# Second expert: the mean's small operation folded into scales, and other pairs with 512-column steps in the second product

## The chip, the cores and the metric

The kernel runs on one core of a Trainium2 chip. The metric is the device time of one execution in microseconds (us). The engines are TensorE (PE in the profile: matmul, with its weight loads as PEld), VectorE (DVE), ScalarE (ACT), GpSimd (POOL) and SyncE (SP), which issues the DMAs.

## The reference

A linear attention is followed by two dense experts. The change is in the second, which takes 4,608 tokens of 512 features, in fp32:

```python
h = x @ w_in                                   # 512 -> 1024
h_max = np.max(h, axis=-1, keepdims=True)
e = np.exp(h - h_max)
sm = e / (np.sum(e, axis=-1, keepdims=True) + 1e-09)
solu = h * sm
mu = np.mean(solu, axis=-1, keepdims=True)
var = np.mean((solu - mu) ** 2, axis=-1, keepdims=True)
ln = (solu - mu) / np.sqrt(var + 1e-06) * g_ln
return (ln @ w_out).astype(np.float32)         # 1024 -> 512
```

## The kernel before

The second expert runs from about 850 us to the end. Its 4,608 tokens go through as 18 pairs (`NU = 18`) of two tiles of 128 tokens; `n` is the tile within the pair. Both of its products are Strassen products: seven products of sums of halves in place of eight, each operand split into a high and a low part, so that one product of fp32 precision is three matmuls, high by high (L204), high by low (L205) and low by high (L206). A pair passes through these steps.

- `prep_second` loads the tokens, forms the sums (GpSimd, L779) and splits them into high (ScalarE, L479) and low (GpSimd, L480).
- `second`, the first product: 42 matmuls of 512 columns. Its seven operand products accumulate in a few PSUM banks, and `H_SEED[u]` picks one of three ways to empty these: by additions on VectorE (L1231, and L1236, which takes the row maximum on the way), by copies on ScalarE (L1241, L1281, L1288), or by a mix. With `H_SEED[u]` 0 or 1, one of the banks is the bank called `sums()`, bank 0.
- `soft(u, n)`, in this order: the negated maximum `nmx` (L1309), Exp with the sum `z` (ScalarE, L1314), the product h times e with its sum `sp` (VectorE, L1317), the negated mean `nmp` (VectorE, L1320), the squared small constant `zz` (ScalarE, L1324), the square of the difference from the mean with its sum `v` (ScalarE, L1326), the variance with `zz` (VectorE, L1328), its power of -1/2 `ry` (GpSimd, L1331), `nmp` times `ry` (GpSimd, L1345), and the normalised row (ScalarE, L1347). The division by z is never carried out, since the norm would remove it again; the small constant is scaled with z instead.
- `permute` and `turned` transpose the result: 16 DMAs per pair (L1365), then transposes of 32 x 32 blocks on VectorE (L1392), operand sums (L1403), high part (ScalarE, L1415), low part (VectorE or GpSimd, L1416). The last pair is transposed on TensorE.
- `second_out`, the second product of the pair two before: 7 operand products of 4 blocks. The flat form has three matmuls of 256 columns per block (84 in all), which are drained by additions of 256 columns (L1476) and copies (L1483 on ScalarE, L1481 on VectorE). The wide form, for pairs with `O_WIDE[u]` that are not among the last two (`TAIL`), has one matmul of 512 columns (L1466: high by both weight parts at once) and one of 256 (L1468). Its banks hold two halves that still have to be added: by `wide` (VectorE L1490 over 512 columns, GpSimd L1492 over 256) or by `fold` (VectorE L1496). And its sums are kept by copies on ScalarE, `keep` (L1500); the first of these copies the first bank into bank 0, on which further matmuls accumulate:

```python
prod(bA, A11, B11)
keep(bB, bA)
prod(bC, S3, T3)
prod(bB, S2, T2, more=True)
```

The order of the instructions is decided when the kernel is built. A list scheduler, `Flow`, holds tasks with an engine, a duration out of the code and a due time `at`. At each step it takes the engine that can start first, and there the startable task with the lowest `at`. The instructions are written out in that order, and each engine runs its own in order. The due times come from numbers such as `SOFT_AT`, `E2_LEAD`, `DMA_LAG`, `TURN_LAG` and `OUT_LAG`; on the chip only the order is left of them, and the semaphores.

## Time and profile before

| | |
|---|---|
| Time, median of 3 runs | 1195.18 us (1194.14 to 1196.62) |
| The profiled execution: its time, its span | 1195.32 us, 1193.4 us |
| Granted TensorE clock, mean | 0.998 |
| TensorE busy | 1177.4 us, 99% |
| VectorE, ScalarE, GpSimd busy | 945.2, 861.8, 740.8 us |
| 850 to 1193.4 us: TensorE, VectorE, ScalarE, GpSimd | 338.88, 295.52, 272.64, 211.94 us |

The span runs from the first instruction to the last, and the time has 1.92 us around it. Busy time says how long an engine had an instruction in work, not whether anyone waited for it. Matmuls overlap in the rows (each is shown for some 0.17 us longer than the step to the next), so TensorE's rate is read from start to start. An idle time in a row stands in front of the instruction, with what ended it.

### The profile page before, as it was taken

The page shows a single profiled execution, that of the slowest core. Times are in us where ns is not written, and L with a number is a line of the kernel's source. Part 1 is how long each engine was busy: PE and PEld are TensorE (multiplying, and loading weights), DVE is VectorE, ACT ScalarE, POOL GpSimd, SP SyncE. Part 2 cuts the span into 40 slices and gives each one's busy share as a digit, 9 for nine tenths or more (in the row PEclk, how much of TensorE's full clock was granted, in tenths as well). Part 3 has the DMA queues.
Part 4 walks back from the last instruction along what each step waited for, and adds up shares of the span by engine and source line. Part 5 has one row for each costly group of instructions (what it writes and reads, how often), then busy time and mean ns, then how long its engine had stood idle before and what let it go on. Part 6 is the DMA issues. An engine that isn't in the chain of part 4 may idle for free.

```text
span 1193.4 us, 20361 instructions
## 1 busy us (share of the span) xinstructions
PE 1177.4 (99%) x6678; PEld 1023.4 (86%) x6678; DVE 945.2 (79%) x1631; ACT 861.8 (72%) x1602; POOL 740.8 (62%) x737
## 2 busy tenths in 40 slices
...
GB/s 321 287 364 330 332 319 326 327 271 302 306 200 215 316 275 228 354 302 219 179 353 313 202 206 336 283 247 333 275 108 117 92 134 79 131 100 100 102 94 54
DMA packets 244394, 281.35 MB, mean 236 GB/s; under 512 B 17984, under 2 KB 169536, under 8 KB 244288
## 3 DMA queue, kind: packets, MB, share of 16 engines
...
q8 instruction: 53, 0.87, 0.3%
q14 instruction: 53, 0.43, 0.1%
...
## 4 chain that ended last, share of the span: by engine, by line
PE 90%; DVE 5%; SPq 2%; ACT 1%; DMA 1%; issue 1%; POOL 0%; DVEq 0%; ACTq 0%
PE ps L204 26%; PE ps L206 26%; PE ps L205 26%; PE ps L1466 4%; PE ps L709 3%; PE ps L1468 2%; PE ps L591 2%; SPq L1365 1%; PE ps L741 1%; DMA att<-qkv 1%; DMA xf<-px 1%; DVE mid L1084 0%; DVE rxa L480 0%; DVE ps L1392 0%; DVE fconv L1403 0%
## 5 line engine op out<-in xcount | busy, mean ns | idle before, releaser
L204 PE MATMUL ps<-rg,rwo 128*128 128x512 f32 (+2 forms) x752 | 269.6, 359 | 2.0 <-DVE fh L1084 1.1
L206 PE MATMUL ps<-rg,rwo 128*128 128x512 f32 (+2 forms) x752 | 265.7, 353 | 0.0
L205 PE MATMUL ps<-rg,rwo 128*128 128x512 f32 (+2 forms) x752 | 265.5, 353 | 0.0
L204 PEld LDWEIGHTS ps<-rg,rwo 128*128 128x128 f32 x752 | 141.7, 188 | 20.7 <-DVE mid L1084 2.7
L206 PEld LDWEIGHTS ps<-rg,rwo 128*128 128x128 f32 x752 | 141.7, 188 | 16.3
L480 POOL TENSOR_TENSOR rg<-rawp,rg 128x512 fp32r<-128x512 f32 (+1 forms) x84 | 116.8, 1402 | 62.0 <-ACT rg L479 58.4
L205 PEld LDWEIGHTS ps<-rg,rwo 128*128 128x128 f32 x752 | 141.9, 189 | 15.0
L204 PE MATMUL ps<-rxa,rwi 128*128 128x512 f32 (+1 forms) x384 | 144.8, 377 | 0.0
L206 PE MATMUL ps<-rxa,rwi 128*128 128x512 f32 (+1 forms) x384 | 144.3, 376 | 0.0
L205 PE MATMUL ps<-rxa,rwi 128*128 128x512 f32 (+1 forms) x384 | 144.3, 376 | 0.0
L840 DVE SCALAR_TENSOR_TENSOR fh<-ps,fh 128x512 f32<-128x512 f32 (+1 forms) x126 | 81.0, 648 | 45.7 <-ACT fh L838 44.0
L843 ACT ACTIVATE fh<-fh,const 128x512 f32<-128x512 f32 (+1 forms) x156 | 105.1, 689 | 16.7 <-DVE fh L840 15.6
L204 PE MATMUL ps<-rxb,rwi 128*128 128x512 f32 (+1 forms) x288 | 109.4, 380 | 1.9 <-DVE fh L948 0.9
L205 PE MATMUL ps<-rxb,rwi 128*128 128x512 f32 (+1 forms) x288 | 108.4, 376 | 0.0
L206 PE MATMUL ps<-rxb,rwi 128*128 128x512 f32 (+1 forms) x288 | 108.3, 376 | 0.0
L480 POOL TENSOR_TENSOR ws<-fconv,ws 128x512 fp32r<-128x512 f32 x68 | 83.3, 1228 | 38.6 <-ACT ws L479 32.7
L479 ACT CAST rg<-rawp 128x512 fp32r<-128x512 f32 (+1 forms) x144 | 83.3, 597 | 27.3 <-PE ps L206 18.9
L838 ACT ACTIVATE fh<-ps 128x512 int32<-128x512 f32 (+1 forms) x126 | 70.6, 566 | 44.1 <-PE ps L206 41.8
L779 POOL TENSOR_TENSOR sf<-xf 128x256 f32<-128x256 f32 x72 | 65.5, 909 | 30.5 <-DMA xf<-xd 22.8
L204 PEld LDWEIGHTS ps<-rxa,rwi 128*128 128x128 f32 x384 | 72.1, 188 | 12.1 <-ACT ps L963 0.4
L206 PEld LDWEIGHTS ps<-rxa,rwi 128*128 128x128 f32 x384 | 72.1, 188 | 11.7
L205 PEld LDWEIGHTS ps<-rxa,rwi 128*128 128x128 f32 x384 | 72.1, 188 | 10.8
(197 smaller groups left out, 3122.1 us busy)
## 6 DMA issues: line engine op xcount, KB each, us to landing
...
fh<-e2n SPq DMA_DIRECT2D x256, 64.0 KB, 2.1
...
```

The lines of the kernel that those rows point to most:

```text
L204: PE.matmul(ps, lhsT=lh, rhs=rh, start=start, stop=False, skip_group_check=more)
L205: PE.matmul(ps, lhsT=lh, rhs=rl, start=False, stop=False, skip_group_check=more)
L206: PE.matmul(ps, lhsT=ll, rhs=rh, start=False, stop=stop, skip_group_check=more)
L479: add("ACT", 0.62 if n == 512 else 0.405, lambda: ACT.copy(out=hi(), in_=src()), r=keys, w=hk, at=at)
L480: either(on_dve, n, lambda eng: eng.tensor_tensor(out=lo(), in0=src(), in1=f(hi()), op=ALU.subtract), [*keys, *hk], lk, at)
L591: PE.matmul(buf[bk][e * D:(e + 1) * D, p % 2 * D:(p % 2 + 1) * D], lhsT=k_[:, at_:at_ + D], rhs=k_[:, v_ + at_:v_ + at_ + D], start=(c == ...
L709: PE.matmul(buf[bk][row:row + n, c], lhsT=buf[qs[p]][:, a:a + n], rhs=buf[kvf][:, c], start=True, stop=True)
L779: add("POOL", 0.74, lambda: POOL.tensor_tensor(out=out_(), in0=in0(), in1=in1(), op=fn), r=[*keys, *r], w=w, at=at)
L838: add("ACT", e_(0.6, 0.385, n), lambda: ACT.activation(out=tt().bitcast(I32), in_=h(), func=AF.Copy, scale=INV_2PI, bias=0.25), r=r, w=[tk ...
L840: add("DVE", e_(0.69, 0.418, n), lambda: DVE.scalar_tensor_tensor(out=tt(), in0=h(), scalar=INV_2PI, in1=tt().bitcast(I32), op0=ALU.mult, ...
L843: add("ACT", e_(0.725, 0.509, n), lambda: ACT.activation(out=tt(), in_=tt(), func=AF.Sin, bias=buf["halfpi"][:, 0:1], scale=TWO_PI), r=[tk ...
L1466: PE.matmul(buf[bk], lhsT=hi, rhs=lw_room(b, c // 2)[:, c % 2, :], start=first, stop=False, skip_group_check=True)
```

## The change

It has three parts.

First, other pairs take the wide form of the second product. Before, these were pairs 2, 5, 6, 7, 8, 10, 11 and 13 (pair 17 has the flag but is among the last two); now they are 3 to 15.

Second, the negated mean is no longer formed. The product h times e carries 1 / FP (FP = 1,024) as its scale, so that its sum `sp` is the mean itself and the stored product is smaller by FP. The later scales take that back: Square has the scale -FP and the bias `sp`, the variance the scale 1 / FP^3, the small constant is divided by FP, and GpSimd's last small operation multiplies `sp` by `ry` and -1 / FP. The variance moves from VectorE to GpSimd (`SMALL_POOL[2]`).

Third, numbers of the scheduler: due times of the second expert, `H_SEED` and `O_SEED` (a flat product's choice of banks).

```diff
-E2_LEAD, SOFT_AT, SOFT_D, Q_OFF, CP_D = -33.18, -44.29, -15.08, -0.17, 6.96
+E2_LEAD, SOFT_AT, SOFT_D, Q_OFF, CP_D = 1.52, -76.41, 31.31, -0.17, 6.96
...
-H_SEED = (2, 2, 0, 0, 0, 2, 0, 0, 2, 0, 0, 0, 0, 0, 0, 0, 0, 0)
+H_SEED = (0, 1, 1, 2, 1, 0, 0, 1, 2, 0, 2, 0, 2, 0, 0, 0, 2, 0)
...
-O_WIDE, MM_W = (0, 0, 1, 0, 0, 1, 1, 1, 1, 0, 1, 1, 0, 1, 0, 0, 0, 1), 0.342
+O_WIDE, MM_W = (0, 0, 0, 1, 1, 1, 1, 1, 1, 1, 1, 1, 1, 1, 1, 1, 0, 0), 0.342
...
-PAIR_C, DMA_LAG, TURN_LAG, OUT_LAG = 58.48, 33.18, 71.85, 121.5
+PAIR_C, DMA_LAG, TURN_LAG, OUT_LAG = 46.11, 17.79, 118.53, 95.24
...
+SMALL_POOL = (0, 0, 1)
...
         if n or H_SEED[u] != 1:
-            add("DVE", 0.15, lambda: DVE.tensor_scalar(out=sm("nmx"), in0=sm("mb"), scalar1=-1.0, scalar2=None,
-                                                       op0=ALU.mult), r=[("mb", n)], w=[("nmx", n)], at=at, ps=True)
+            eng, dur = ("POOL", 0.2) if SMALL_POOL[0] else ("DVE", 0.15)
+            add(eng, dur, lambda: (POOL if eng == "POOL" else DVE).tensor_scalar(
+                out=sm("nmx"), in0=sm("mb"), scalar1=-1.0, scalar2=None, op0=ALU.mult),
+                r=[("mb", n)], w=[("nmx", n)], at=at, ps=True)
...
-        add("DVE", 1.3, lambda: DVE.scalar_tensor_tensor(out=buf[hk], in0=buf[hk], scalar=1.0, in1=buf[ek],
+        add("DVE", 1.3, lambda: DVE.scalar_tensor_tensor(out=buf[hk], in0=buf[hk], scalar=1.0 / FP, in1=buf[ek],
...
-        add("DVE", 0.15, lambda: DVE.tensor_scalar(out=sm("nmp"), in0=sm("sp"), scalar1=-1.0 / FP, scalar2=None,
-                                                  op0=ALU.mult), r=[("sp", n)], w=[("nmp", n)], at=at, ps=True)
...
+        add("ACT", 1.24, lambda: ACT.activation(out=buf["junk"], in_=buf[hk], func=AF.Square, scale=-float(FP),
+                                                bias=sm("sp")[:, 0:1], accum_out=sm("v")),
+            r=[hk, ("sp", n)], w=[("v", n), "junk"], at=at)
...
+        def var(eng):
+            return lambda: eng.tensor_scalar(out=sm("v"), in0=sm("v"), scalar1=1.0 / FP ** 3, scalar2=sm("zz")[:, 0:1],
+                                             op0=ALU.mult, op1=ALU.add)
+
+        eng, dur = ("POOL", 0.2) if SMALL_POOL[2] else ("DVE", 0.16)
+        add(eng, dur, var(POOL if SMALL_POOL[2] else DVE), r=[("v", n), ("zz", n)], w=[("v", n)], at=at, ps=True)
...
+        add("POOL", 0.2, lambda: POOL.tensor_scalar(out=sm("nmp"), in0=sm("sp"), scalar1=sm("ry")[:, 0:1], scalar2=-1.0 / FP,
+                                                    op0=ALU.mult, op1=ALU.mult),
+            r=[("ry", n), ("sp", n)], w=[("nmp", n)], at=at, ps=True)
```

Two lines of `soft` use one variable: the function that issues `nmx` reads `eng` when the scheduler runs it, and by then `eng` has been set anew, to "POOL", for the variance. The scheduler has planned `nmx` on VectorE, and the order shows it on GpSimd (L1310) in 32 of the 36 cases; in the other four it is a reduction on VectorE. Lines of the changed kernel stand 1 to 14 lower in the code: Exp is L1316, the product L1319, Square L1331, the variance L1336, the power L1341, `keep` L1510, and from `permute` on every line is 10 further down.

The order at three places shows what moves. The first is the softmax of pair 12. `const_5_73` is the tile with all the small values, `edge_0_133` the one with the maxima, `fconv_0_103` holds h and e, and `ps0_0_169` is bank 0. On GpSimd before:

```order
L779 TENSOR_TENSOR sf_0_107<-xf_0_112 128x256 [waits DMAHW5_49]
L480 TENSOR_TENSOR rwi0_0_731<-sf_1_108,rwi0_0_731 128x512 [waits PE_49,Activation_49]
L779 TENSOR_TENSOR sf_0_107<-sf_0_107,xf_0_112 128x256 [waits DMAHW2_49,Pool_49]
L779 TENSOR_TENSOR sf_0_107<-xf_0_112 128x256
L779 TENSOR_TENSOR sf_0_107<-xf_0_112,sf_0_107 128x256 [waits Pool_49]
L480 TENSOR_TENSOR rwi0_0_731<-xf_1_113,rwi0_0_731 128x256 [waits PE_49,Activation_49]
L1331 TENSOR_TENSOR const_5_73<-const_5_73,const_2_70 128x1 [waits DVE_49]
L1345 TENSOR_TENSOR const_5_73<-const_5_73 128x1 [waits Pool_49]
```

GpSimd in the change, at the same place:

```order
L480 TENSOR_TENSOR rwi0_0_731<-xf_1_113,rwi0_0_731 128x512 [waits PE_49,Activation_49]
L480 TENSOR_TENSOR rwi0_0_731<-sf_1_108,rwi0_0_731 128x512 [waits PE_49,Activation_49]
L1310 TENSOR_SCALAR const_5_73<-edge_0_133 128x1 [waits DVE_49]
L480 TENSOR_TENSOR rwi0_0_731<-sf_1_108,rwi0_0_731 128x512 [waits PE_49,Activation_49]
L1310 TENSOR_SCALAR const_5_73<-edge_0_133 128x1 [waits DVE_49]
L1336 TENSOR_SCALAR const_5_73<-const_5_73 128x1 [waits Activation_49]
L1341 TENSOR_TENSOR const_5_73<-const_5_73,const_2_70 128x1 [waits Pool_49]
L1358 TENSOR_SCALAR const_5_73<-const_5_73 128x1 [waits DVE_49,Pool_49]
```

Two negated maxima (L1310), which wait for VectorE, and the variance (L1336) now stand on GpSimd among the subtractions. ScalarE before, at the two Exps of that pair and the copy into bank 0 (L1500):

```order
L1314 ACTIVATE fconv_0_103,const_5_73<-fconv_0_103,const_5_73 128x1024 [waits DVE_49,Activation_49,Pool_49]
L1324 ACTIVATE const_5_73<-const_5_73,const_1_69 128x1 [waits Activation_49]
L1314 ACTIVATE fconv_0_103,const_5_73<-fconv_0_103,const_5_73 128x1024 [waits DVE_49]
L1500 COPY ps0_0_169<-ps1_0_173 128x512 [waits PE_49]
L1324 ACTIVATE const_5_73<-const_5_73,const_1_69 128x1 [waits Activation_49]
L1326 ACTIVATE fconv_0_103,const_5_73<-fconv_0_103,const_5_73 128x1024 [waits DVE_49]
```

ScalarE in the change:

```order
L1316 ACTIVATE fconv_0_103,const_5_73<-fconv_0_103,const_5_73 128x1024 [waits Activation_49,Pool_49]
L1329 ACTIVATE const_5_73<-const_5_73,const_1_69 128x1 [waits Activation_49]
L1316 ACTIVATE fconv_0_103,const_5_73<-fconv_0_103,const_5_73 128x1024 [waits Pool_49]
L1510 COPY ps0_0_169<-ps7_0_197 128x512 [waits PE_49]
L1331 ACTIVATE fconv_0_103,const_5_73<-fconv_0_103,const_5_73 128x1024 [waits DVE_49]
L1281 COPY fh_0_117<-ps6_0_193 128x512 [waits PE_49]
```

Exp waits for GpSimd in place of VectorE, and the copy into bank 0 (now L1510) still stands behind both Exps here. Over the wide products of the whole kernel, this copy stood ahead of both Exps in 1 case, between them in 4 and behind both in 3; in the change in 1, 7 and 5.

The second place is VectorE at the softmax of pair 12. Before:

```order
L1236 ISA fconv_0_103,edge_0_133<-ps7_0_197,fh_0_117,edge_0_133 128x512 [waits DVE_49,PE_49]
L1236 ISA edge_0_133 128x1
L1309 TENSOR_SCALAR const_5_73<-edge_0_133 128x1 [waits DVE_49]
L1416 TENSOR_TENSOR e2r_1_7847<-ps5_0_189,e2r_1_7847 128x512 [waits Activation_49]
L1236 ISA fconv_0_103,edge_0_133<-ps0_0_169,fh_0_117,edge_0_133 128x512 [waits PE_49]
L1236 ISA edge_0_133 128x1
L1309 TENSOR_SCALAR const_5_73<-edge_0_133 128x1 [waits DVE_49]
L1317 SCALAR_TENSOR_TENSOR fconv_0_103,const_5_73<-fconv_0_103 128x1024 [waits Activation_49]
L1320 TENSOR_SCALAR const_5_73<-const_5_73 128x1 [waits DVE_49,Pool_49]
L1317 SCALAR_TENSOR_TENSOR fconv_0_103,const_5_73<-fconv_0_103 128x1024 [waits Activation_49]
L1320 TENSOR_SCALAR const_5_73<-const_5_73 128x1 [waits DVE_49,Pool_49]
L1328 SCALAR_TENSOR_TENSOR const_5_73<-const_5_73 128x1 [waits Activation_49]
```

VectorE in the change:

```order
L1236 ISA fconv_0_103,edge_0_133<-ps6_0_193,fh_0_117,edge_0_133 128x512 [waits DVE_49,PE_49,Pool_49]
L1236 ISA edge_0_133 128x1
L1426 TENSOR_TENSOR e2r_2_7860<-ps3_0_181,e2r_2_7860 128x512
L1236 ISA fconv_0_103,edge_0_133<-ps0_0_169,fh_0_117,edge_0_133 128x512 [waits DVE_49,PE_49,Pool_49]
L1236 ISA edge_0_133 128x1
L1319 SCALAR_TENSOR_TENSOR fconv_0_103,const_5_73<-fconv_0_103 128x1024 [waits Activation_49]
L1402 STREAM_TRANSPOSE ps2_0_177<-fh_0_117 128x512 [waits DMAHW4_49,DMAHW5_49,DMAHW3_49,DMAHW6_49,DMAHW2_49,DMAHW7_49,DMAHW1_49,DMAHW0_49]
L1319 SCALAR_TENSOR_TENSOR fconv_0_103,const_5_73<-fconv_0_103 128x1024 [waits DVE_49,Activation_49]
L1402 STREAM_TRANSPOSE ps3_0_181<-fh_0_117 128x512
L1506 TENSOR_REDUCE e2n_3_7454<-ps7_0_197 128x256 [waits PE_49]
```

The operations L1309, L1320 and L1328 have left VectorE, and the product of the second tile (L1319) stands behind a transpose that waits for the transfers of `permute`.

The third is TensorE at the second product of pair 3, which was flat. Before, in its first operand product:

```order
L206 MATMUL ps6_0_193<-rxb_0_2622,rwi0_0_731 128x512
L204 MATMUL ps7_0_197<-rg_0_87,rwo_0_77 128x256 [waits DVE_49]
L205 MATMUL ps7_0_197<-rg_0_87,rwo_0_77 128x256
L206 MATMUL ps7_0_197<-rg_0_87,rwo_0_77 128x256
L204 MATMUL ps7_0_197<-rg_0_87,rwo_0_77 128x256
L205 MATMUL ps7_0_197<-rg_0_87,rwo_0_77 128x256
```

TensorE in the change, in the first operand product of the same pair:

```order
L205 MATMUL ps0_0_169<-rxb_0_2622,rwi0_0_731 128x512
L206 MATMUL ps0_0_169<-rxb_0_2622,rwi0_0_731 128x512
L1476 MATMUL ps6_0_193<-rg_0_87,rwo_0_77 128x512
L1478 MATMUL ps6_0_193<-rg_0_87,rwo_0_77 128x256
L1476 MATMUL ps6_0_193<-rg_1_88,rwo_0_77 128x512
L1478 MATMUL ps6_0_193<-rg_1_88,rwo_0_77 128x256
```

Three matmuls of 256 columns per block have become one of 512 and one of 256, and the first product's matmuls (into `ps0`) stand between the blocks. TensorE has 140 fewer instructions in all, 28 for each of five pairs.

## Rows read from the trace of the kernel before

**Rows 1.** The page, busy time: us (share of the span) and instructions.
```profile
PE 1177.4 (99%) x6678; PEld 1023.4 (86%) x6678; DVE 945.2 (79%) x1631; ACT 861.8 (72%) x1602; POOL 740.8 (62%) x737
```

**Rows 2.** Windows: busy us (instructions) of each engine, PEclk, DMA share, GB/s.
```profile
860.00:1180.00 320.00, 318.99 (x1864) 280.81 (x1863) 284.90 (x593) 260.95 (x473) 202.55 (x234) 1.00 0.37 103
```

**Rows 3.** Timeline of TensorE, a flat product's ends: start, duration, instruction, [idle].
```profile
922.48 0.28 PE L204 MATMUL ps<-rg,rwo 128*128 128x256 f32 x1
...
932.55 0.40 PE L204 MATMUL ps<-rxb,rwi 128*128 128x512 f32 x1
```

**Rows 4.** Timeline of TensorE, 24 matmuls of a wide product.
```profile
985.65 0.39 PE L1466 MATMUL ps<-rg,rwo 128*128 128x512 f32 x1
...
989.88 0.40 PE L204 MATMUL ps<-rxb,rwi 128*128 128x512 f32 x1
```

**Rows 5.** Timeline of TensorE around its three longest gaps in the second expert.
```profile
860.46 0.39 PE L206 MATMUL ps<-rxa,rwi 128*128 128x512 f32 x1
861.51 0.50 PE L204 MATMUL ps<-rxb,rwi 128*128 128x512 f32 x1 [0.67 <-DVE edge L1236]
861.85 0.39 PE L205 MATMUL ps<-rxb,rwi 128*128 128x512 f32 x1
...
901.39 0.28 PE L1468 MATMUL ps<-rg,rwo 128*128 128x256 f32 x1
901.86 0.50 PE L204 MATMUL ps<-rxb,rwi 128*128 128x512 f32 x1 [0.19 <-DVE edge L1236]
...
1116.98 0.28 PE L1468 MATMUL ps<-rg,rwo 128*128 128x256 f32 x1
1117.40 0.50 PE L204 MATMUL ps<-rxb,rwi 128*128 128x512 f32 x1
```

**Rows 6.** Groups of VectorE, 800 to 1193.4: busy, mean ns | idle before.
```profile
L1392 DVE STREAM_TRANSPOSE ps<-fh 128x512 f32<-128x512 f32 x64 | 42.6, 706 | 2.2 <-issue 1.4 <-DMA xf<-px 0.5 <-DMA fh<-e2n 0.3
...
L1476 DVE TENSOR_TENSOR fh<-ps,e2n 128x256 f32<-128x256 f32 x25 | 10.4, 418 | 9.4 <-PE ps L206 6.6 <-ACT e2n L1483 2.8
...
L1490 DVE TENSOR_TENSOR e2n<-ps,e2n 128x512 f32<-128x512 f32 x16 | 10.9, 679 | 1.5 <-ACT e2n L1500 1.4
...
L1328 DVE SCALAR_TENSOR_TENSOR const<-const 128x1 f32<-128x1 f32 x36 | 7.0, 202 | 4.1 <-ACT fconv L1326 3.9
...
L1320 DVE TENSOR_SCALAR const<-const 128x1 f32<-128x1 f32 x36 | 5.2, 151 | 2.6
```

**Rows 7.** Groups of ScalarE, the same stretch.
```profile
L1314 ACT ACTIVATE fconv<-fconv,const 128x1024 f32<-128x1024 f32 x36 | 41.4, 1151 | 12.7 <-DVE const L1309 12.4
...
L1500 ACT COPY e2n<-ps 128x512 f32<-128x512 f32 x16 | 9.2, 575 | 1.0 <-PE ps L1468 0.9
```

**Rows 8.** Groups of GpSimd, the same stretch.
```profile
L480 POOL TENSOR_TENSOR rwi<-sf,rwi 128x512 fp32r<-128x512 f32 x35 | 45.4, 1308 | 10.7 <-ACT rwi L479 10.5
...
L1345 POOL TENSOR_TENSOR const<-const 128x1 f32<-128x1 f32 x36 | 6.8, 190 | 2.8
...
L1492 POOL TENSOR_TENSOR fh<-e2n 128x256 f32<-128x256 f32 x8 | 5.9, 741 | 4.8 <-DVE e2n L1490 4.3 <-DVE const L1328 0.4
```

**Rows 9.** Timeline of VectorE ahead of the gap at 860.46.
```profile
857.41 0.47 DVE L1328 SCALAR_TENSOR_TENSOR const<-const 128x1 f32<-128x1 f32 x1
```

**Rows 10.** Timeline of ScalarE, then TensorE, at pair 12: the copy into bank 0.
```profile
1060.93 1.14 ACT L1314 ACTIVATE fconv<-fconv,const 128x1024 f32<-128x1024 f32 x1
...
1062.07 0.58 ACT L1500 COPY ps<-ps 128x512 f32<-128x512 f32 x1
...
1063.07 0.40 PE L1466 MATMUL ps<-rg,rwo 128*128 128x512 f32 x1
```

**Rows 11.** Timeline of GpSimd, then VectorE, at the same place.
```profile
1060.11 0.74 POOL L779 TENSOR_TENSOR sf<-sf,xf 128x256 f32<-128x256 f32 x1
1060.80 1.75 POOL L779 TENSOR_TENSOR sf<-xf 128x256 f32<-128x256 f32 x1
...
1060.73 1.23 DVE L1317 SCALAR_TENSOR_TENSOR fconv<-fconv 128x1024 f32<-128x1024 f32 x1
```

40 lines of the change are left out of this document (18 added, 22 removed).

## The prediction

> **What bounds the kernel now.** I read the page first: TensorE is busy for 99% of the span [rows 1]. Between 860 and 1180 us, which is the second expert almost alone, TensorE is busy for 318.99 of 320 us at the full granted clock (1.00, the 2.4 GHz level); VectorE follows with 284.90, ScalarE with 260.95, GpSimd with 202.55 [rows 2]. The other engines therefore count only by the moments at which TensorE waits for one of them. So I went through TensorE's own timeline for gaps between matmuls. A 256-column matmul takes 0.12 us from start to start (10.07 us for the 84 of one second product [rows 3]) and a 512-column one about 0.23 (a pair of both takes 4.23 / 12 = 0.353 [rows 4]). Against that, three gaps of any size stand in the second expert [rows 5]: 860.46 to 861.51 (1.05 us, so 0.82 too much), 901.39 to 901.86 (0.35 too much) and 1116.98 to 1117.40 (0.30 too much). The matmul behind such a gap is slow as well: 861.51 to 861.85 is 0.34, 0.11 too much, which I take for all three. The first two name a VectorE drain of PSUM (L1236) as releaser. All three together are 1.8 us: this is all that relief of VectorE can be worth at these places.
>
> **The second product in 512-column steps.** A flat product is 7 x 4 x 3 = 84 matmuls of 256 columns, a wide one 28 of 512 and 28 of 256: the same 21,504 columns in 56 instructions. Eight pairs were wide, thirteen are now: five products change. Per twelve flat matmuls the trace has 10.07 / 7 = 1.439 us [rows 3], for the eight that replace them 4.23 / 3 = 1.410 [rows 4]. The difference of 0.029 times 7 operand products times 5 pairs is **-1.0 us**. Only one product of each kind stands behind it, so I keep 0 and -2.0 as bounds.
>
> The Trainium skill ("TensorE: Matmul & The Clock Gate", Back-to-back issue gap) gives an isolated matmul N / 2.4 ns plus some 2.5 ns at the warm clock. By that estimate the 28 instructions saved per product would be worth 28 x 2.5 = 70 ns, 0.35 us for five products in place of 1.0. The trace has 120 ns where this formula has 109, so it is the trace that I follow.
>
> **The same products on the other engines.** On VectorE 29 additions of 256 columns (L1476, 0.418) and a net two more copies turn into 10 additions (L1490) and 10 folds of 512 columns at some 0.68 [rows 6]: -12.1 + 0.8 + 13.6 = +2.3 us. ScalarE gets 15 more copies of 512 columns (L1500, 0.575) and 23 - 10 more in the first product, whose drains were dealt out anew by H_SEED: 28 x 0.575 = 16.1, less 8 short copies [rows 7], so about +13. GpSimd gets 10 additions of 0.741 (L1492) [rows 8]. None of it takes time at these totals, since ScalarE stays near 274 of 320 us and TensorE is at 319.
>
> **The mean.** The operation that made the negative mean (L1320, 36 x 0.151 = 5.4 us) is gone, the variance sum (L1328, 36 x 0.202 = 7.3) goes to GpSimd, and so does, as the order shows, the negated maximum (L1309, of the size of L1320, 32 of 36; the other four become a reduction over 1,024 columns) [rows 6]. VectorE loses 36 x (0.151 + 0.151 + 0.202) = 18.1 us here, +2.3 above, and 18 half-bank operations of the first product (18 x 0.68 = 12.2), less the four reductions at twice 0.68 (5.4): -22.6 us, so 262 of 320. Also gone are its waits ahead of these operations, 4.1 us before L1328 and 2.6 before L1320 [rows 6], which delayed what stood behind. GpSimd gains 68 operations of 0.19 (as L1345 [rows 8]) = 12.9, and 7.4: 223 of 320 us, a share of 0.70.
>
> What is that relief worth? In front of the gap at 860.46 VectorE did a variance sum from 857.41 that took 0.47 instead of 0.20 because it waited, and the drains behind it came late [rows 9]. Without it I take this gap as gone: 0.93 with its slow matmul. The two others (0.35 + 0.30 + 0.22 = 0.87) stand behind runs of half-bank work that the new seeds deal out otherwise; I take half, 0.43. Together **-1.4 us**, bounds 0 and -1.8.
>
> **What the move of the negated maximum adds.** Exp (L1314) waits for that maximum and already stands 12.4 us in all for it [rows 7]. On VectorE it stood directly behind the drain that makes it. On GpSimd, in order, it stands behind whatever GpSimd has begun: at pair 12 a subtraction L480, which takes 1.308 [rows 8]. Behind Exp on ScalarE stands the copy that keeps a product in bank 0 (L1500) and behind that the matmul that writes on there. In pair 12 the second Exp ran from 1060.93, the copy from 1062.07 for 0.58, so to 1062.65, and the first matmul on the kept sum began at 1063.07, only 0.42 us later [rows 10]. If GpSimd is busy with 0.70 and the rest of the operation in front is anything between 0 and 1.3 us, the part beyond 0.42 is on average 0.88 x 0.88 / (2 x 1.3) = 0.30, times 0.70 = 0.21 us per pair. That hits where the copy stands behind both Exps, in 5 of the 13 pairs by the order; where it stands between the two (7), an Exp of 1.14 us is no longer ahead of it, and I take nothing. 5 x 0.21 = **+1.0 us**. And where the maximum stands at the head of GpSimd's queue before the drain is done, the subtractions L480 queued behind it wait too, and after them the first product's matmul with the low part; with 30% of GpSimd's time free I take nothing for it. Bounds: 0, where GpSimd is free in time, and 12 x 0.88 = 10.6, where it always waits out a whole L480.
>
> The order of the permuting transfers and of the VectorE transposes behind them changes as well. VectorE's 64 transposes stood idle for 2.2 us in all, of which 0.8 for transfers [rows 6]. In the change the second half's L1319 stands behind such a transpose at pair 12, and behind it that half's Square, norm and permute. I put it at nothing, since both results are wanted two pairs later only, and keep its loss as a rival.
>
> **Sum.** -1.0 - 1.4 + 1.0 = -1.4 us against the profiled execution's 1195.32 (span 1193.4 and 1.92 around it): 1193.9. The median of the runs is 0.14 below the profiled one, which changes nothing.
>
> **Rivals.**
> *The relief is whole, and GpSimd is free.* All 1.8 us of gaps go, the maximum costs nothing: -1.0 - 1.8 = -2.8, so 1192.5 or somewhat less. For it: VectorE falls from 89% to 82% of the window, and Exp no longer queues behind VectorE's other work. Against it: the gaps are three accidents of order, and a new order may have others.
> *The maximum on GpSimd delays what stands behind it (the other side).* If Exp comes late by enough that the kept bank comes 0.43 us late in each of 12 pairs, TensorE stands 5.2 us more, and with the 1.0 saved and no relief the time is 1199.5. It is slower by over 0.2% (2.4 us, which is about what a measurement of this kernel can tell from no change) from (2.4 + 1.0) / 12 = 0.28 us per pair. For it: GpSimd's additions (L779) take 0.74 at 1060.11, but 1.75 at 1060.80, when VectorE's two-input product L1317 began at 1060.73 [rows 11]. A maximum for the second half that is ready just there, behind such an operation, would wait out the product too. Against it: ScalarE has other work to do meanwhile, and 7 of 13 copies moved ahead of the second Exp.
> The Trainium skill ("SBUF — State Buffer", Who interferes with whom) says of the same: a VectorE operation with two SBUF inputs and a GpSimd operation that reads SBUF exclude each other for a whole instruction. The trace agrees, 0.74 against 1.75; by it the delay would be the rest of the product, up to 1.2 us.
> *The gain is given back at the transposes.* If VectorE stands for late permutes by 0.13 us in each of 18 pairs and TensorE behind it, the 2.4 us saved are gone: 1195.2.
>
> **How the numbers follow.** The forecast has 0.40; its own range is 1192.3 to 1195.5 (0.07 of it below the bound for faster, 0.33 within). The whole relief has 0.33, all faster. The late maximum has 0.15, 0.13 of it slower and 0.02 within. The transposes have 0.12: 0.10 within, 0.02 slower. So faster 0.40, same 0.45, slower 0.15. The range of 1191.2 to 1197.4 takes in the forecast, the transposes, most of the whole relief (with two us saved by the wide products instead of one) and the late maximum where it costs up to 0.25 us per pair.
>
> **What would show it.** Twelve flat matmuls replaced by eight at 1.41; TensorE's gaps of 0.82, 0.35 and 0.30 gone or elsewhere; VectorE near 262 us in the window; negated maxima on GpSimd that begin up to 1.3 us behind the drain; ScalarE's idle time before Exp above 12.4 us; the copy into bank 0 ending closer than 0.42 to its matmul, and gaps on L1476 where it ends behind. The prediction is wrong if such gaps, or new ones behind transposes and casts, sum to more than 3.5 us, or if the wide products save more than 0.06 us for each twelve.

## The result

The changed kernel takes 1202.57 us (median of 4 runs, 1200.74 to 1202.75), the kernel before in the same comparison 1194.66 (1193.57 to 1196.62): ratio 1.0063, interval 1.0050 to 1.0076, so 7.9 us slower. The profiled execution is the quickest of the four (1200.74 us, span 1199.0), 1.8 below the median. In nine of the sixteen profiled executions of this document, that of the kernel before among them but not that of the changed one, TensorE's granted clock is 0.50 (the 1.2 GHz level) for 3.4 us near 26 us, which makes them some 1.6 us longer. The kernel before in its window from 26 to 29 us:

```profile
26.00:29.00 3.00, 3.00 (x26) 2.36 (x25) 2.37 (x6) 1.63 (x5) 0.00 (x0) 0.50 1.05 325
```

The same window of the changed kernel has 1.00; from 20 to 25 us TensorE was busy for 3.23 us in both, so what sets the clock there stays open. So traces are compared from 740 us on: from the 4,201st matmul, the same one in all these orders, to the last, TensorE takes 449.3 us before and 456.9 in the change. That is 7.5 us of the 7.9.

### The profile after

The page's busy times, against [rows 1]:

```profile
PE 1179.3 (98%) x6538; PEld 1014.7 (85%) x6538; DVE 925.8 (77%) x1499; ACT 873.5 (73%) x1622; POOL 759.0 (63%) x815
```

The windows from 860 to 1180 us, against [rows 2]:

```profile
860.00:1180.00 320.00, 316.07 (x1678) 267.67 (x1679) 264.23 (x467) 269.04 (x486) 218.28 (x304) 1.00 0.38 107
```

The other engines came out as forecast: VectorE 264 us (forecast 262, before 285), ScalarE 269 (274), GpSimd 218 (223). TensorE is busy for 316.1 of 320 us in place of 319.0 and gets through less in it (685,056 columns against 695,808), at the same granted clock (1.00, the 2.4 GHz level). So the time went into waits of TensorE, which the next lines look for.

The term for the wide products came out as well. From TensorE's timeline, the first of 24 matmuls of a wide product and the one behind the last:

```profile
924.13 0.39 PE L1476 MATMUL ps<-rg,rwo 128*128 128x512 f32 x1
...
928.36 0.40 PE L1476 MATMUL ps<-rg,rwo 128*128 128x512 f32 x1
```

4.23 us for 24, so 1.41 for eight as in [rows 4]: five products save their 1.0 us. What else happens is in the gaps. I took each step of TensorE from start to start, from 780 us on, and summed what it has over the normal step (0.226 us after 512 columns, 0.120 after 256, 0.109 after 128), where that is above 0.025. The kernel before has 3.0 us of this and the changed one 11.1.

The groups of ScalarE, Exp, against [rows 7], and of GpSimd, the negated maximum and the last small operation:

```profile
L1316 ACT ACTIVATE fconv<-fconv,const 128x1024 f32<-128x1024 f32 x36 | 41.3, 1148 | 15.6 <-POOL const L1310 14.3 <-POOL rwo L1426 0.7 <-DVE const L1314 0.3
```

```profile
L1310 POOL TENSOR_SCALAR const<-edge 128x1 f32<-128x1 f32 x32 | 10.1, 315 | 12.6 <-DVE edge L1236 11.2 <-DVE edge L1257 0.8 <-DMA fh<-e2n 0.3
...
L1358 POOL TENSOR_SCALAR const<-const 128x1 f32<-128x1 f32 x36 | 9.4, 260 | 3.8
```

ScalarE's idle time before Exp has gone from 12.7 to 15.6 us, 14.3 of it for GpSimd. What that does is seen at single places. The timeline of GpSimd, VectorE, ScalarE and TensorE around 853 us:

```profile
850.05 1.30 POOL L480 TENSOR_TENSOR rwi<-sf,rwi 128x512 fp32r<-128x512 f32 x1
851.31 1.21 POOL L1310 TENSOR_SCALAR const<-edge 128x1 f32<-128x1 f32 x1
...
850.01 0.75 DVE L1236 CUSTOM_DVE_ANT_0 fconv<-ps,fh,edge 128x512 f32<-128x512 f32 x1 [0.30 <-issue]
...
850.69 1.74 DVE L1319 SCALAR_TENSOR_TENSOR fconv<-fconv 128x1024 f32<-128x1024 f32 x1
...
852.56 1.15 ACT L1316 ACTIVATE fconv<-fconv,const 128x1024 f32<-128x1024 f32 x1 [1.54 <-POOL const L1310]
...
853.70 0.58 ACT L1241 COPY ps<-ps 128x512 f32<-128x512 f32 x1
...
853.12 0.40 PE L206 MATMUL ps<-rxa,rwi 128*128 128x512 f32 x1
854.33 0.50 PE L204 MATMUL ps<-rxa,rwi 128*128 128x512 f32 x1 [0.82 <-ACT ps L1241]
```

The maximum of the second half, ready when VectorE's drain L1236 ended at 850.76, stood behind a subtraction until 851.31 and then took 1.21 us, where the others take about 0.23: VectorE's product with two SBUF operands (L1319) had run since 850.69, and both ended at 852.4 to 852.5. ScalarE stood idle for 1.54 us before Exp, the copy into bank 0 behind it ended at 854.28, and TensorE had the gap: 0.99 us, and 0.11 in the slow matmul behind. Three of the 32 maxima on GpSimd (at 851.31, 984.94 and 1125.17) took 1.11 to 1.21 us, each while such a product ran, the other 29 took 0.21 to 0.27. The Trainium skill ("SBUF — State Buffer", Who interferes with whom) says that a VectorE instruction with two SBUF inputs contends with a GpSimd instruction that reads SBUF; this trace agrees (1.21 against 0.23).

The same engines around 1085 us, without VectorE:

```profile
1082.36 1.30 POOL L480 TENSOR_TENSOR rwi<-sf,rwi 128x512 fp32r<-128x512 f32 x1 [0.60 <-ACT rwi L479]
1083.63 0.23 POOL L1310 TENSOR_SCALAR const<-edge 128x1 f32<-128x1 f32 x1
...
1083.89 1.15 ACT L1316 ACTIVATE fconv<-fconv,const 128x1024 f32<-128x1024 f32 x1 [1.61 <-POOL const L1310]
...
1085.37 0.58 ACT L1510 COPY ps<-ps 128x512 f32<-128x512 f32 x1
1085.88 1.14 ACT L1316 ACTIVATE fconv<-fconv,const 128x1024 f32<-128x1024 f32 x1
...
1085.42 0.28 PE L1478 MATMUL ps<-e2r,e2r 128*128 128x256 f32 x1
1086.00 0.50 PE L1476 MATMUL ps<-rg,rwo 128*128 128x512 f32 x1 [0.30 <-ACT ps L1510]
```

Here no such product ran. The maximum waited out a subtraction of 1.30 us, Exp began at 1083.89, the copy ended at 1085.95, and TensorE's matmul on the kept sum began 0.46 us late, with a slow step behind it. The trace has six gaps behind a late Exp (853, 946, 987, 1007, 1085, 1164): 2.7 us with their slow matmuls. At the last of them (0.15) GpSimd was idle, and the maximum ran as soon as VectorE's drain had ended. Four of them (946, 1007, 1085, 1164) stand where the copy is between the two Exps of a pair, as it is at 1085.37 above, and one (987) where it is behind both.

### The profile page after: what moved, and what is told of

The parts are those of the page before. It is cut to its first block, busy times and chain, and to the rows that moved or that the text cites. A ratio compares the mean times of both kernels' runs of the same rounds, so it can differ in the third digit from the quotient of the medians.

```text
span 1199.0 us, 20054 instructions
## 1 busy us (share of the span) xinstructions
PE 1179.3 (98%) x6538; PEld 1014.7 (85%) x6538; DVE 925.8 (77%) x1499; ACT 873.5 (73%) x1622; POOL 759.0 (63%) x815
## 4 chain that ended last, share of the span: by engine, by line
PE 89%; DVE 4%; ACT 3%; POOL 1%; issue 1%; DMA 1%; SPq 0%; ACTq 0%; DVEq 0%; POOLq 0%
PE ps L204 25%; PE ps L206 25%; PE ps L205 25%; PE ps L1476 6%; PE ps L1478 3%; PE ps L709 3%; PE ps L591 2%; PE ps L741 1%; ACT fconv L1316 1%; DMA att<-qkv 1%; DVE mid L1084 0%; ACT e2n L1361 0%; DVE rxa L480 0%; DVE rxb L480 0%; SPq L1375 0%
## 5 line engine op out<-in xcount | busy, mean ns | idle before, releaser
L204 PE MATMUL ps<-rg,rwo 128*128 128x512 f32 (+2 forms) x672 | 246.7, 367 | 1.9 <-DVE mid L1084 0.8
L206 PE MATMUL ps<-rg,rwo 128*128 128x512 f32 (+2 forms) x672 | 243.2, 362 | 0.6 <-DVE rwo L1426 0.6
L205 PE MATMUL ps<-rg,rwo 128*128 128x512 f32 (+2 forms) x672 | 242.8, 361 | 0.0
L480 POOL TENSOR_TENSOR rg<-rawp,rg 128x512 fp32r<-128x512 f32 (+1 forms) x84 | 116.0, 1392 | 62.3 <-ACT rg L479 59.7
L204 PEld LDWEIGHTS ps<-rg,rwo 128*128 128x128 f32 x672 | 126.4, 188 | 20.3 <-DVE mid L1084 2.2
L206 PEld LDWEIGHTS ps<-rg,rwo 128*128 128x128 f32 x672 | 126.4, 188 | 16.9 <-DVE rwo L1426 0.8
L205 PEld LDWEIGHTS ps<-rg,rwo 128*128 128x128 f32 x672 | 126.5, 188 | 14.8
L480 POOL TENSOR_TENSOR ws<-fconv,ws 128x512 fp32r<-128x512 f32 x68 | 83.8, 1236 | 38.5 <-ACT ws L479 32.3
L479 ACT CAST rg<-rawp 128x512 fp32r<-128x512 f32 (+1 forms) x144 | 83.5, 597 | 25.0 <-PE ps L206 20.2
L462 POOL TENSOR_TENSOR fconv<-fconv 128x512 int32<-128x512 int32 x40 | 53.5, 1338 | 43.4 <-DVE fconv L455 34.6
```

What stands on the lines that cost most here:

```text
L204: PE.matmul(ps, lhsT=lh, rhs=rh, start=start, stop=False, skip_group_check=more)
L205: PE.matmul(ps, lhsT=lh, rhs=rl, start=False, stop=False, skip_group_check=more)
L206: PE.matmul(ps, lhsT=ll, rhs=rh, start=False, stop=stop, skip_group_check=more)
L462: add("POOL", 1.3, lambda: POOL.tensor_tensor(out=buf[wk].bitcast(I32), in0=buf[yk].bitcast(I32), in1=buf[wk].bitcast(I32), op=ALU.add), r ...
L479: add("ACT", 0.62 if n == 512 else 0.405, lambda: ACT.copy(out=hi(), in_=src()), r=keys, w=hk, at=at)
L480: either(on_dve, n, lambda eng: eng.tensor_tensor(out=lo(), in0=src(), in1=f(hi()), op=ALU.subtract), [*keys, *hk], lk, at)
```

## The experiments

Theory 1 puts the loss down to the negated maximum on GpSimd, theory 2 to the new order itself. Each run is timed in five rounds against the kernel before on the same chip. The intervals of the ratios are 1 to 2 us wide to either side, so a difference of under 2 us between two runs is shown by their traces or not at all.

### The maximum taken back: a_nmx_dve

```diff
-            add(eng, dur, lambda: (POOL if eng == "POOL" else DVE).tensor_scalar(
+            add(eng, dur, lambda eng=eng: (POOL if eng == "POOL" else DVE).tensor_scalar(
```

> The changed kernel with the negated maximum back on VectorE, in the place where its scheduler had planned it; the order of TensorE, ScalarE and the DMAs stays that of the change word for word. Theory 1 (the maximum on GpSimd makes Exp and the copy into bank 0 behind it late): the loss of 7.5 us goes, and with the 1.0 saved by the wide products the time is 1193 to 1195, ratio to the kernel before 0.998 to 1.001. Theory 2 (the new order itself, its first-product copies L1241 and due times, stalls TensorE): it stays at 1200 or more, ratio 1.005.

Measured: 1198.9 us (1197.91 to 1200.54), ratio 1.0034 (1.0022 to 1.0046). It lies between the two. Each against the kernel before of its own comparison, the maximum on GpSimd costs 7.9 - 4.4 = 3.5 us, and 4.4 stay. The intervals leave the 3.5 anything from 1 to 6; by the traces from the 4,201st matmul on it is 2.4 (456.9 - 454.4), and by the gaps 2.7. The group of Exp on ScalarE:

```profile
L1316 ACT ACTIVATE fconv<-fconv,const 128x1024 f32<-128x1024 f32 x36 | 41.3, 1148 | 6.8 <-DVE const L1310 5.2 <-POOL rwo L1426 0.6 <-DVE ps L1413 0.3
```

Exp's idle time falls to 6.8 us, and the six gaps are gone. Others remain. From the timelines of this run, TensorE at pair 8, then ScalarE and TensorE near the end:

```profile
978.73 0.39 PE L206 MATMUL ps<-rxa,rwi 128*128 128x512 f32 x1
979.79 0.50 PE L204 MATMUL ps<-rxa,rwi 128*128 128x512 f32 x1 [0.68 <-ACT fh L1241]
...
1165.19 1.15 ACT L1331 ACTIVATE fconv<-fconv,const 128x1024 bf16<-128x1024 f32 x1
...
1166.34 1.23 ACT L1361 ACTIVATE e2n<-fconv,const 128x1024 f32<-128x1024 f32 x1
1167.47 0.56 ACT L1510 COPY e2n<-ps 128x512 f32<-128x512 f32 x1
...
1166.74 0.28 PE L1478 MATMUL ps<-rg,rwo 128*128 128x256 f32 x1
1168.09 0.50 PE L1476 MATMUL ps<-e2r,e2r 128*128 128x512 f32 x1 [1.07 <-ACT e2n L1510]
```

At 978.73 the first product of pair 8 (H_SEED 2) goes on in the bank that it has just filled, which ScalarE must copy first: 0.84 us over the normal step. At 1166.74 the wide product of pair 15 goes on in bank 0, and the copy that keeps it (L1510) stands behind Square and the normalised row: 1.23 us.

### The maximum moved in the old order: b_nmx_pool

```diff
-            add("DVE", 0.15, lambda: DVE.tensor_scalar(out=sm("nmx"),
+            add("DVE", 0.15, lambda: POOL.tensor_scalar(out=sm("nmx"),
```

> The kernel before with its 36 negated maxima issued on GpSimd where its scheduler planned them on VectorE; nothing else moves. Theory 1: the loss appears here as well, 4 to 8 us, ratio 1.003 to 1.007, with TensorE's gaps behind the copy into bank 0. Theory 2: within 2 us of before, ratio 0.999 to 1.002.

Measured: 1196.6 us (1195.31 to 1197.56), ratio 1.0014 (1.0005 to 1.0022): 2.1 us slower, less than theory 1 asked for, at the edge of what theory 2 allowed. GpSimd, VectorE and ScalarE at 851, then VectorE and TensorE at 860, then ScalarE and TensorE at 965:

```profile
850.55 1.12 POOL L1309 TENSOR_SCALAR const<-edge 128x1 f32<-128x1 f32 x1 [0.33 <-DVE edge L1236]
...
850.38 1.22 DVE L1317 SCALAR_TENSOR_TENSOR fconv<-fconv 128x1024 f32<-128x1024 f32 x1
...
851.70 1.15 ACT L1314 ACTIVATE fconv<-fconv,const 128x1024 f32<-128x1024 f32 x1 [0.84 <-POOL const L1309]
...
857.66 0.69 DVE L1403 TENSOR_TENSOR fconv<-ps,fconv 128x512 f32<-128x512 f32 x1 [0.61 <-ACT fconv L1427]
...
858.92 0.39 PE L206 MATMUL ps<-rxa,rwi 128*128 128x512 f32 x1
860.79 0.50 PE L204 MATMUL ps<-rxb,rwi 128*128 128x512 f32 x1 [1.49 <-DVE edge L1236]
...
962.09 1.15 ACT L1314 ACTIVATE fconv<-fconv,const 128x1024 f32<-128x1024 f32 x1 [1.60 <-POOL const L1309]
...
964.38 0.57 ACT L1500 COPY ps<-ps 128x512 f32<-128x512 f32 x1
...
964.54 0.40 PE L206 MATMUL ps<-rxb,rwi 128*128 128x512 f32 x1
965.00 0.50 PE L1466 MATMUL ps<-rg,rwo 128*128 128x512 f32 x1
```

The gap of [rows 5] grows from 0.82 to 1.65. The way there leads through ScalarE: the maximum at 850.55 took 1.12 us while VectorE's product L1317 ran, Exp began behind it at 851.70, and after Exp come the squares, the normalised row (L1347) and a copy (L1427), for which VectorE's four half-bank operations ahead of the drain still wait 0.61 us at 857.66. At 964.54 Exp, behind an idle time of 1.60, delays the copy into bank 0, and a gap of 0.23 is new. The move costs 2.1 us in this order (1.7 by the traces) and 3.5 in the new one (2.4); that the order around it makes the difference is not shown, since the intervals overlap.

### The folded mean in the old order: b_fold and b_fold_v

Both take the folded mean and keep the order of TensorE, ScalarE and the DMAs (the place of the removed operation stays in the plan, empty). b_fold also has the variance on GpSimd.

```diff
-        add("DVE", 0.15, lambda: DVE.tensor_scalar(out=sm("nmp"), in0=sm("sp"), scalar1=-1.0 / FP, scalar2=None,
-                                                  op0=ALU.mult), r=[("sp", n)], w=[("nmp", n)], at=at, ps=True)
+        add("DVE", 0.15, lambda: None, r=[("sp", n)], w=[("nmp", n)], at=at, ps=True)
...
-        add("DVE", 0.16, lambda: DVE.scalar_tensor_tensor(out=sm("v"), in0=sm("v"), scalar=1.0 / FP, in1=sm("zz"),
+        add("DVE", 0.16, lambda: POOL.tensor_scalar(out=sm("v"), in0=sm("v"), scalar1=1.0 / FP ** 3, scalar2=sm("zz")[:, 0:1],
```

> The kernel before with the folded mean and the variance on GpSimd, but the negated maximum still on VectorE, and the order of TensorE, ScalarE and the DMAs kept as it was. By the relief term of the prediction VectorE's waits ahead of the gap at 860 go: 0 to 1.8 us saved, ratio 0.9985 to 1.000. By theory 2 no loss either. If small operations on GpSimd cost anything by themselves, it is slower.

Measured: 1194.9 us (1193.54 to 1200.29), ratio 1.0008 (0.9998 to 1.0018): no difference is shown, and the gain that the relief term asked for is not there. The gaps at 901 and 1117 are gone, and the one at 860 has grown. ScalarE, VectorE and TensorE there:

```profile
859.85 1.24 ACT L1347 ACTIVATE e2n<-fconv,const 128x1024 f32<-128x1024 f32 x1 [0.75 <-POOL const L1344]
...
861.12 0.69 DVE L1236 CUSTOM_DVE_ANT_0 fconv<-ps,fh 128x512 f32<-128x512 f32 x1 [0.55 <-ACT e2n L1347]
...
860.26 0.39 PE L206 MATMUL ps<-rxa,rwi 128*128 128x512 f32 x1
861.88 0.50 PE L204 MATMUL ps<-rxb,rwi 128*128 128x512 f32 x1 [1.23 <-DVE edge L1236]
```

The drain L1236 now waits 0.55 us for the normalised row (L1347), since it writes where that one still reads. And that one comes 0.5 us later than in the kernel before, whose row is this, as variance, power and product now all stand on GpSimd among its additions:

```profile
859.38 1.24 ACT L1347 ACTIVATE e2n<-fconv,const 128x1024 f32<-128x1024 f32 x1
```

> The kernel before with the folded mean alone: the operation for the negative mean is gone, the variance and the negated maximum stay on VectorE, and the order of TensorE, ScalarE and the DMAs is kept. By the relief term of the prediction, 0 to 1.8 us faster, ratio 0.9985 to 1.000. By the reading of the run with the variance on GpSimd, in which the gap at 860 grew because the norm came 0.5 us later, the gap at 860 is 0.83 or less here and those at 901 and 1117 go: 0.3 to 0.9 us faster.

Measured: 1193.52 us (1192.36 to 1194.52), ratio 0.9993 (0.9984 to 1.0002): 0.9 us faster, as expected, though the interval still holds 1. TensorE at 860:

```profile
860.21 0.39 PE L206 MATMUL ps<-rxa,rwi 128*128 128x512 f32 x1
861.19 0.50 PE L204 MATMUL ps<-rxb,rwi 128*128 128x512 f32 x1 [0.59 <-DVE edge L1236]
```

0.75 us over the normal step; the gaps at 901 and 1117 are gone, as in b_fold. So by the gaps it is the removed operation that helps, 0.7 us in all, and the variance on GpSimd gives that back at 860 (1.39 in place of 0.75). The times agree with it, but their intervals overlap.

Why the gap at 860 stays is seen in the kernel before. Behind the variance sum of [rows 9], which ended at 857.88, VectorE went on with this:

```profile
858.37 0.69 DVE L1403 TENSOR_TENSOR fconv<-ps,fconv 128x512 f32<-128x512 f32 x1 [0.48 <-ACT fconv L1427]
```

It stood idle for 0.48 us more, for a copy on ScalarE (L1427) that comes behind the squares and a normalised row there. From then on it has no pause up to the drain. In b_fold_v it waits 0.68 us for that copy. The variance's wait was covered by a longer one.

### Other lists of wide pairs in the kernel before: b_wide13, b_wide_mid, b_wide_9_14, b_wide_9

```diff
-O_WIDE, MM_W = (0, 0, 1, 0, 0, 1, 1, 1, 1, 0, 1, 1, 0, 1, 0, 0, 0, 1), 0.342
+O_WIDE, MM_W = (0, 0, 0, 1, 1, 1, 1, 1, 1, 1, 1, 1, 1, 1, 1, 1, 0, 0), 0.342
...
+O_WIDE, MM_W = (0, 0, 1, 1, 1, 1, 1, 1, 1, 1, 1, 1, 1, 1, 0, 0, 0, 0), 0.342
...
+O_WIDE, MM_W = (0, 0, 1, 0, 0, 1, 1, 1, 1, 1, 1, 1, 0, 1, 1, 0, 0, 0), 0.342
...
+O_WIDE, MM_W = (0, 0, 1, 0, 0, 1, 1, 1, 1, 1, 1, 1, 0, 1, 0, 0, 0, 1), 0.342
```

> The kernel before with the change's list of wide pairs alone (3 to 15), planned anew by the scheduler with the old due times. By the term of the prediction 1.0 us saved by five more wide products, ratio 0.999, if its new order brings no gaps. By theory 2, in which an order decides by its own accidents, it can be a few us slower, with new gaps behind the copies into bank 0.

Measured: 1198.83 us (1197.72 to 1201.0), ratio 1.0036 (1.0024 to 1.0048): 4.3 us slower, by this list alone. The saving is there, the new order costs more.

> The kernel before with wide products for pairs 2 to 13, so four more in the middle and none at the end. Theory 1: what cost 4.3 us in the run with pairs 3 to 15 were the last two (gaps of 1.0 at 1112.3, 1.2 at 1152.7, and 1.5 at 1160.9 to 1166.9), so it is 0.5 to 1 us faster than before: ratio 0.999 to 1.000. Theory 2 (a wide product costs wherever it is put): about 2 us slower, ratio 1.002.

Measured: 1198.66 us (1197.99 to 1200.1), ratio 1.0036 (1.0023 to 1.0048). Both expectations missed: it is not the end alone, and 4.6 us is more than theory 2 said. VectorE and TensorE at the largest gap:

```profile
1053.28 0.69 DVE L1403 TENSOR_TENSOR ps<-ps,fconv 128x512 f32<-128x512 f32 x1
1053.88 0.68 DVE L1490 TENSOR_TENSOR e2n<-ps,e2n 128x512 f32<-128x512 f32 x1
1054.48 0.68 DVE L1403 TENSOR_TENSOR fconv<-fconv,ps 128x512 f32<-128x512 f32 x1
1055.07 1.41 DVE L1231 TENSOR_TENSOR fh<-ps,fh 128x512 f32<-128x512 f32 x2
...
1054.46 0.40 PE L206 MATMUL ps<-rxa,rwi 128*128 128x512 f32 x1
1055.81 0.50 PE L204 MATMUL ps<-rxa,rwi 128*128 128x512 f32 x1 [0.96 <-DVE fh L1231]
```

TensorE's order at this place says why:

```
4969 L204 MATMUL ps0_0_169<-rxa_0_82,rwi0_0_731 128x512
4970 L205 MATMUL ps0_0_169<-rxa_0_82,rwi0_0_731 128x512
4971 L206 MATMUL ps0_0_169<-rxa_0_82,rwi0_0_731 128x512
4972 L204 MATMUL ps0_0_169<-rxa_1_83,rwi0_0_731 128x512 [waits DVE_49]
```

Two operand products of the first product stand one behind the other in bank 0 (`ps0`), and between them VectorE has to empty the bank (L1231), behind the sums L1403 and an addition. I read it so that a wide product keeps its sums in bank 0 too, and pushes the first product's shares of that bank together. This became theory 3: a bank written twice running, with a drain between, costs TensorE about 1 us. I counted such places in the orders of the second expert: none in the kernel before, 3 in b_wide13, 4 in b_wide_mid, 2 in the changed kernel, 5 in a_seed_b, 4 in a_tail_seed (both below).

> The kernel before with two more wide products, pairs 9 and 14, chosen by the order alone: in it TensorE never writes two blocks in a row into one bank with a drain between them, which it does four times with pairs 2 to 13 wide and three times with 3 to 15. Theory 3 (each such repeat costs TensorE the length of the drain and its queue, 0.84 to 1.23 us, and nothing else is wrong with wide products): no gap near 1 us appears and the time is 0 to 0.5 us below before, ratio 0.999 to 1.001. If wide products cost by themselves, some 0.8 us each as in the two runs before: 1196 and above, ratio 1.0013 or more.

Measured: 1200.04 us (1199.03 to 1202.03), ratio 1.0050 (1.0036 to 1.0063). Theory 3's time is missed by far, and the time alone would fit wide products that cost by themselves. But up to 1166 us no gap is new, as theory 3 has it; the loss stands at the end. ScalarE and TensorE there:

```profile
1166.28 1.24 ACT L1347 ACTIVATE e2n<-fconv,const 128x1024 f32<-128x1024 f32 x1 [0.52 <-POOL const L1345]
...
1166.26 0.28 PE L206 MATMUL ps<-ws,e2r 128*128 128x256 f32 x1
1168.71 0.71 PE L1380 MATMUL ps<-const,e2n 128*128 128x128 f32 x4 [2.17 <-ACT e2n L1347]
```

TensorE's order now puts the transposes of the last pair ahead of the second product of pair 16, and they wait for the normalised row: 2.33 us, and 2.26 for the next four at 1169.09. Behind these two waits the granted clock is 0.50 (the 1.2 GHz level) up to 1176 us, which adds some 2 us to TensorE's steps.

> The kernel before with one more wide product, pair 9, and pair 14 flat; no bank is written twice running with a drain between. If the loss of the run with 9 and 14 (5.6 us) stood at the end alone, as its two gaps of 2.3 us say, the time is that of before or up to 0.5 us below, ratio 0.999 to 1.001. If a wide product in the middle costs by itself, 1195.5 or above.

Measured: 1194.38 us (1192.97 to 1196.77), ratio 1.0000 (0.9991 to 1.0008). One more wide product in the middle costs nothing. Its 0.2 us are too little to be told.

### The end and the seeds of the changed kernel: a_tail_flat, a_seed_b, a_tail_seed

These three and the next two also have the edit of a_nmx_dve.

```diff
-O_WIDE, MM_W = (0, 0, 0, 1, 1, 1, 1, 1, 1, 1, 1, 1, 1, 1, 1, 1, 0, 0), 0.342
+O_WIDE, MM_W = (0, 0, 0, 1, 1, 1, 1, 1, 1, 1, 1, 1, 1, 1, 0, 0, 0, 0), 0.342
...
-H_SEED = (0, 1, 1, 2, 1, 0, 0, 1, 2, 0, 2, 0, 2, 0, 0, 0, 2, 0)
+H_SEED = (2, 2, 0, 0, 0, 2, 0, 0, 2, 0, 0, 0, 0, 0, 0, 0, 0, 0)
```

> The changed kernel with the negated maximum on VectorE (1198.9 us) and pairs 14 and 15 flat again, as before the change; its plan is the same up to the product of pair 14. In the run with the maximum on VectorE the product of pair 15, which has no first product left to stand between its blocks, shows gaps of 0.17, 1.23 and 0.11 behind the kept sums. Theory 1 (wide products at the end are exposed): these go, and 1.5 to 2.5 us with them, less 0.4 for two flat products: 1197 to 1198. Theory 2 (the loss is in the seeds and due times): 1199 or more.

Measured: 1197.56 us (1196.4 to 1199.2), ratio 1.0028 (1.0018 to 1.0038): 0.9 us back (4.4 - 3.5), the gaps of pair 15 are gone. The intervals overlap; by the traces from the 4,201st matmul on it is 1.6. 3.5 us of loss stay, by the medians and by the traces.

> The changed kernel with the negated maximum on VectorE and the H_SEED of the kernel before, planned anew. Theory 1 (end): the time stays within 1 us of 1198.9. Theory 2 (the copies L1241 of the pairs with seeds 1 and 2, behind which TensorE stood 0.84, 0.63 and 0.76 at 978.7, 1017.3 and 863.8): these gaps go, 2 us or more faster, 1197 or below.

Measured: 1205.69 us (1204.97 to 1206.66), ratio 1.0095 (1.0080 to 1.0111). Both missed. The old seeds do take the old gaps away, but in this order they bring one of 4.0 us at 859 and five of 0.94 to 1.23 at the five repeats. The large one is no repeat: TensorE waits for a cast of the first product's operand on ScalarE (L479). Behind it the granted clock is low for a while:

```profile
863.00:866.00 3.00, 2.84 (x7) 2.29 (x8) 1.38 (x6) 2.55 (x6) 2.90 (x3) 0.50 0.31 76
```

At 0.50, the 1.2 GHz level, matmuls of 512 columns step by 0.43 us in place of 0.226, which costs 1.5 us more.

> Both of the last two at once: pairs 14 and 15 flat, H_SEED of before, the maximum on VectorE. If both theories hold side by side, the savings add up and the time is 1195 or less. If it stays above 1197, the due times of the first expert's end and of the second are what is left.

Measured: 1204.3 us (1203.38 to 1205.24), ratio 1.0081 (1.0069 to 1.0094). The savings do not add up. The flat end saves 1.4 against a_seed_b (1.5 by the traces); the gap of 4.0 us stays.

### Two orders picked by their repeats: a_nmx_plan, a_lag

```diff
-SMALL_POOL = (0, 0, 1)
+SMALL_POOL = (1, 0, 1)
...
-PAIR_C, DMA_LAG, TURN_LAG, OUT_LAG = 46.11, 17.79, 118.53, 95.24
+PAIR_C, DMA_LAG, TURN_LAG, OUT_LAG = 46.11, 17.79, 118.53, 91.24
```

> The change with its scheduler told that the negated maximum runs on GpSimd, planned anew. If the loss of that move (3.7 us) came from the plan not knowing of it, the time is 1199 or less. By theory 3 it is not: the new order has five repeats of a bank with a drain between, against two in the change, so three more gaps of about 1 us, 1203 or above if nothing else falls away.

Measured: 1206.54 us (1205.7 to 1207.61), ratio 1.0104 (1.0090 to 1.0118). Slower, as theory 3 said; the five repeats have gaps of 0.84 to 1.34. A sixth, at 865.72, where both operand products read the same tile (`rxb`), has 1.21; and three places that are none have 0.95, 1.73 and 1.33 (863, 1174, 1179). That the scheduler knows where the maximum runs is no help.

> The changed kernel with the negated maximum on VectorE and pairs 14 and 15 flat (1197.6 us), and one due time of the second product (OUT_LAG) 4 us earlier, planned anew. Its order has four repeats of a bank with a drain between, against one. Theory 3: three more gaps of 0.8 to 1.2 us, 1199.5 to 1201. If repeats do not decide, within 1 us of 1197.6.

The lines of a_tail_flat are in this run too. Measured: 1215.21 us (1213.82 to 1217.01), ratio 1.0177 (1.0163 to 1.0191). The time that theory 3 gave is missed by 14 us. The four repeats have their gaps, 0.84 to 0.85 each, but 14 us more come from others: three of 1.55 before bank 0's kept sum, one of 3.2 at the end. So each repeat has its gap, and theory 3 says nothing of other places; 4 us in one due time moved the time by 17 us.

### The two that help, together: b_fold_w9

The edits of b_fold_v and b_wide_9.

> The same with the folded mean, all small operations left on VectorE: the 0.9 us of the run b_fold_v and the 0.2 us of one wide product add up, ratio 0.998 to 0.9995. If one takes the other's cover away, 1.000 or above.

Measured: 1192.95 us (1192.13 to 1195.04), ratio 0.9991 (0.9982 to 0.9999). It is the fastest of all: 1.5 us below the kernel before by the medians, 1.1 by the ratio, which is just clear of no change, and 0.6 by the traces from the 4,201st matmul on, about as much as b_fold_v (0.7). That the two edits add up is not shown.

## Why the prediction was wrong

**The step that failed** is the order. The prediction asked of the new due times and seeds only what they do to the three old gaps ("the new seeds deal out otherwise; I take half"), and let a new order's own gaps stand as a remark against a rival ("a new order may have others"). No term of the sum had them, although the part on the change showed that most of the second expert was planned anew. They are the largest term: with the maximum back on VectorE 4.4 us are still lost (a_nmx_dve), 5.4 with the 1.0 that the wide products save. The prediction's own sign of being wrong, new gaps of more than 3.5 us, came about. All kernels, sorted by time (TensorE's excess from the profiled execution, as above):

| kernel | median against before, us | excess, us | repeats |
|---|---|---|---|
| b_fold_w9 | -1.5 | 2.5 | 0 |
| b_fold_v | -0.9 | 2.3 | 0 |
| b_wide_9 | 0.0 | 3.0 | 0 |
| before | 0 | 3.0 | 0 |
| b_fold | +0.4 | 2.9 | 0 |
| b_nmx_pool | +2.1 | 4.6 | 0 |
| a_tail_flat | +3.5 | 6.4 | 1 |
| b_wide13 | +4.3 | 8.1 | 3 |
| a_nmx_dve | +4.4 | 8.5 | 2 |
| b_wide_mid | +4.6 | 8.7 | 4 |
| b_wide_9_14 | +5.6 | 9.4 | 0 |
| changed kernel | +7.9 | 11.1 | 2 |
| a_tail_seed | +10.2 | 13.4 | 4 |
| a_seed_b | +11.6 | 15.4 | 5 |
| a_nmx_plan | +12.1 | 16.4 | 6 |
| a_lag | +20.8 | 23.7 | 4 |

The excess, less 3.0 and what the wide products save, gives every time to within 0.8 us. All 31 repeats of these orders have a gap, of 0.84 to 1.34 us; that they come from the wide products' sums in bank 0 is a reading of the order, not shown by itself.

Term by term:
- Wide products, -1.0: right as a rate (1.41 for eight).
- Relief of VectorE, -1.4: in the old order the removed operation gives 0.9 (b_fold_v; 0.7 by the gaps, and not clear of noise), as the gaps at 901 and 1117 go. The gap that I took as gone, at 860, stays at 0.75. The wait was misread: behind the variance sum VectorE stood 0.48 us longer for ScalarE's copy L1427. With the variance on GpSimd the normalised row, which reads what the drain overwrites, is later and the gap longer (1.39 in b_fold). That step was wrong, and the whole relief with it (rival 1).
- The maximum on GpSimd, +1.0: the mechanism was right, the size and the places were not. It costs 3.5 us (2.4 by the traces). It was priced by half an L480 in the 5 of 13 pairs with the copy behind both Exps; of these one has a gap (987, 0.33 with its slow matmul). The 7 pairs with the copy between the Exps were put at nothing, since "an Exp of 1.14 us is no longer ahead of it"; but the first Exp still is, and four of them have gaps (1.2 together). I had given the wait behind L1319 to the rival only, and the first product's copies (853, 1.1) to nobody. Rival 2, which named that wait, had 5.2 for all of it.
- Transposes on VectorE (rival 3): VectorE's idle time before them is 1.4 us, before 2.2; nothing was given back there.
- The busy times of the other engines came out as forecast, but that bore on nothing: none of them was the limit.

So of the 7.9 us, 3.5 are the maximum's by the medians (2.4 by the traces), shown by a_nmx_dve, and 0.9 (1.6) those of the wide products at the end, whose gaps are gone in a_tail_flat. The remaining 3.5 (with the 0.6 that three wide products save, 4.1 of loss) lie in gaps that can be named, here at their times in a_nmx_dve: at the end of the first expert (803 and 820, 1.2 us with their slow matmuls), between 857 and 865 (2.0, where the kernel before has 0.9 at 860), in pair 8 (0.95), and at 1017 and 1059 (1.1). Which of the due times and seeds makes each of these stays mostly open: the one seed swap (a_seed_b) brought others. Of the first two something can be said. The change also moves due times of the first expert's last product (`S_AL`, `S_BL`, `S_DL`) and the start of the second (`E2_AT`), which the part on the change leaves out. The gap at 803 (0.4) is in all seven orders with the change's due times, whichever seeds they have, and in none with the old ones. The one at 820 (0.8) is in the five with the change's seeds as well, and not in a_seed_b and a_tail_seed.
